# Windowed attention with a gated output layer on one core: global rows stored in one transfer per piece of columns, the last accumulator filled, copied and stored in two halves

## The chip, the cores and the metric

The kernel runs on one core of a Trainium2 chip. The metric is the device time of one execution in microseconds; of several runs the median counts.

## What is computed

For 8 batches and 8 heads of 64 channels there are 512 local tokens and 32 global ones. Local queries see local keys at a distance of at most 32 and all global keys; global queries see everything. The 8 heads' outputs stand side by side as x, with 512 columns and 32 + 512 rows per batch, and pass a gated layer:

```python
k_all = np.concatenate([k_g, k_l], axis=2)
out_g = np.matmul(sm(scale * np.matmul(q_g, k_all.transpose(0, 1, 3, 2))), v_all)
mask = np.abs(pos[:, None] - pos[None, :]) <= 32
...
x = concatenate([out_g, out_l], axis=2)   # then (batch, row, 512)
gate = sigmoid(sum_k conv_w[k] * x shifted down by 4 - k rows)
out = (gate * (x @ w_val)) @ w_out
```

The output has 8 batches of 544 rows of 512 f32. In each batch the first 32 rows belong to the global tokens.

## The kernel before

The work is cut into 32 units, one per batch and pair of heads. For each unit the tensor engine (PE) makes the scores, VectorE (DVE) their minima with the mask, ScalarE (ACT) the exponentials, PE transposes and multiplies by v; DVE and ACT then norm the result and build the gate from it. After four units a batch has all of x, and the function `moe` runs its layer: the tasks g1 (x times w_val, accumulators `pv`), gv (times the gate), gh and gl (the product split into a high and a low part), g2 (times w_out, accumulators `po`), ob (copy of a finished accumulator from PSUM to SBUF) and st (store to DRAM). Each matmul step is three matmuls, high by high, high by low and low by high, in a format that keeps enough bits of f32 together.

The rows of the global tokens of all 8 batches, 256 in number, are gathered in one tile and pass the layer in a last call of `moe` with the key "g". Its names in the profile end in g: `pvg`, `ghg`, `glg`, `pog`, `obg`. It has 48 matmuls of 256 columns in g1, and in g2 two accumulators of 128 rows by 512 columns, r = 0 and 1, with 12 matmuls of 512 columns each (line 643). Rows 0 to 31 of such an accumulator belong to one batch, 32 to 63 to the next, and so on, so four batches share one. A PSUM accumulator of 512 f32 columns comes from the pool's tag "mm", which has two buffers.

The first accumulator is copied by ScalarE alone (line 649). The last one is copied by ScalarE, left 256 columns, and by VectorE, right 256 columns (line 651). `store_g` (lines 834 to 836) then writes four pieces of 32 rows, one per batch, 64 KB each: two issued by SyncE (SP) and two by ScalarE, each queue one after the other. A transfer started on ScalarE's queue takes ScalarE's own time while it is issued.

What sets the order: the string ORDER lists the names of all tasks, and the program is emitted in just this order; each engine works off its instructions in the order in which they were emitted. The costs given to `plan.add` don't change the order. Semaphore waits are placed by the layer that records the program, from the tiles that an instruction reads and writes. The tail of ORDER is the last line of the string: `gl.g.2 gl.g.3 g2.g.0.1 ... g2.g.1.3 ob.g.1 st.g.1`.

Of the kernel before, what the change touches and what calls it, by code (L numbers as in the profile page):

```python
# [8 lines left out]
F32 = mybir.dt.float32  # L9
# [8 lines left out]
B, H, SL, SG, D = 8, 8, 512, 32, 64  # L18
DM = H * D
KW = 5  # L20
P = 128
NDT = DM // P
# [110 lines left out]
g2.7.2.2 st.7.1 gconv2 g2.7.2.3 gconv3 g2.7.3.0 ob.7.2 g2.7.3.1 g2.7.3.2 gconv1 g2.7.3.3 g1.g.0.0 gxl3 gconv0 ob.7.3  # L133
g1.g.0.1 g1.g.0.2 g1.g.0.3 g1.g.1.0 sigg g1.g.1.1 g1.g.1.2 gv.g.0 g1.g.1.3 gh.g.0 g1.g.2.0 gv.g.1 g1.g.2.1 g1.g.2.2
st.7.2 g1.g.2.3 gl.g.0 gv.g.2 gh.g.1 st.7.3 g1.g.3.0 gh.g.2 gl.g.1 g1.g.3.1 g1.g.3.2 g1.g.3.3 gv.g.3 gh.g.3 g2.g.0.0
gl.g.2 gl.g.3 g2.g.0.1 g2.g.0.2 g2.g.0.3 g2.g.1.0 ob.g.0 g2.g.1.1 st.g.0 g2.g.1.2 g2.g.1.3 ob.g.1 st.g.1
"""
E1 = D + 1
PW = "x"
# [6 lines left out]
WO = 2  # L146
NPC = 3
KEEP = 900
LAG = {"PE": 250, "ACT": 160, "DVE": 110, "POOL": 150, "SP": 100, "DMA": 2000, "FREE": 0}
OWN = {"ACT": 100, "DVE": 120}  # L150
PAIR = {("mx", "exp"): -490, ("exp", "t"): 150, ("tc", "av"): -350, ("mx", "mx"): 0, ("gmax", "gmax"): 0, ("halo", "conv"): 40, ("ob", "st"): 30}
# [7 lines left out]
def kind(name):  # L159
    return name.rstrip("0123456789.")  # L160
# [11 lines left out]
class Plan:  # L172
# [17 lines left out]
    def lag(self, d, t):  # L190
# [3 lines left out]
        eng = self.tasks[d].eng  # L194
        return PAIR.get((kind(d), kind(t.name)), OWN.get(eng, 0) if eng == t.eng else LAG[eng])

    def order(self):
# [7 lines left out]
        def put(t):  # L205
# [11 lines left out]
            if kind(t.name) in ("iq", "iv", "wi"):  # L217
                at = max(at, free["PE"] + LAG["PE"])
            if t.eng == "PE":
# [9 lines left out]
            for name, key in t.give:  # L229
                self.rings[name][2][key] = t.end + LAG[t.eng]  # L230
            line.append(t)
# [13 lines left out]
def attention_moe(ctx, tc, qk, vw, maskd, w_val, convT, w_out, out):  # L245
    nc = tc.nc
    V, A, G, T = nc.vector, nc.scalar, nc.gpsimd, nc.tensor

    cp = ctx.enter_context(tc.tile_pool(name="cp", bufs=1))
    sb = ctx.enter_context(tc.tile_pool(name="sb", bufs=2))  # L250
    ps = ctx.enter_context(tc.tile_pool(name="ps", bufs=1, space=PSUM))

    plan = Plan()
# [17 lines left out]
    wvh, wvl, woh, wol = (cp.tile([P, NDT, DM], F32R, name=n) for n in ("wvh", "wvl", "woh", "wol"))  # L271
# [36 lines left out]
    def on_pe(ins):  # L308
        last_pe[:] = [ins.ins]
# [156 lines left out]
    st = {}  # L466
# [137 lines left out]
    def sigmoid(g):  # L604
        A.activation(out=g, in_=g, func=AF.Sigmoid)
# [5 lines left out]
    def moe(key, n, x0, deps_x, deps_gate, before, store):  # L611

        box = {}
        last = before

        def g1(e, t):
            xh, xl = xs_h[x0 + t], xs_l[x0 + t]
            if t == 0:
                box["pv", e] = ps.tile([P, n], F32, tag="mm", name=f"pv{key}_{e}", bufs=2)
            for q, (w, x) in enumerate(((wvh, xh), (wvh, xl), (wvl, xh))):  # L620
                on_pe(T.matmul(box["pv", e], w[:, e, t * P:t * P + P], x, start=(t == 0 and q == 0),  # L621
                         stop=(t == NDT - 1 and q == 2)))

        def gv(e):
            if e == 0:
                box["gh"] = sb.tile([P, NDT, n], F32R, tag="gh", name=f"gh{key}", bufs=1)
                box["gl"] = sb.tile([P, NDT, n], F32R, tag="gl", name=f"gl{key}", bufs=1)
            box["gv", e] = sb.tile([P, n], F32, tag="gv", name=f"gv{key}_{e}")
            V.tensor_tensor(out=box["gv", e], in0=box["pv", e], in1=gates[x0 + e], op=ALU.mult)  # L629

        def gh(e):
            A.copy(box["gh"][:, e, :], box["gv", e])  # L632

        def gl(e):
            V.tensor_tensor(out=box["gl"][:, e, :], in0=box["gv", e], in1=box["gh"][:, e, :].bitcast(F32),
                            op=ALU.subtract)

        def g2(r, e):
            if e == 0:
                box["po", r] = ps.tile([P, DM], F32, tag="mm", name=f"po{key}_{r}", bufs=2)  # L640
            rs = slice(r * P, r * P + P)
            for q, (g, w) in enumerate(((box["gh"], woh), (box["gh"], wol), (box["gl"], woh))):
                on_pe(T.matmul(box["po", r], g[:, e, rs], w[:, e, :], start=(e == 0 and q == 0),  # L643
                         stop=(e == NDT - 1 and q == 2)))

        def ob(r):
            box["ob", r] = sb.tile([P, DM], F32, tag="ob", name=f"ob{key}_{r}")
            at = DM // 2 if (key, r) == ("g", n // P - 1) else DM
            A.copy(box["ob", r][:, :at], box["po", r][:, :at])  # L649
            if at < DM:  # L650
                V.tensor_copy(box["ob", r][:, at:], box["po", r][:, at:])

        part = 700 * n // 512 + (20 if n < 512 else 0)
        early = [f"pc{u}.{KW - 1}" for u in range(NPC)] if key == 0 else []
        for e in range(NDT):
            for t in range(NDT):
                name = f"g1.{key}.{e}.{t}"
                plan.add(name, "PE", part, lambda e=e, t=t: g1(e, t), [last, f"w{e}"] + deps_x(t) + early,
                         take=[("mm", name[:-2])] if t == 0 else [],
                         give=[("xh", x0 + t), ("xl", x0 + t)] if e == NDT - 1 else [])  # L660
                last = name
            plan.add(f"gv.{key}.{e}", "DVE", 620 * n // 512, lambda e=e: gv(e), [last] + deps_gate(e),
                     take=[("gv", f"{key}.{e}")] + ([("g", key)] if e == 0 else []),
                     give=[("mm", f"g1.{key}.{e}"), ("gate", x0 + e)])
            plan.add(f"gh.{key}.{e}", "ACT", 515 * n // 512, lambda e=e: gh(e), [f"gv.{key}.{e}"])
            plan.add(f"gl.{key}.{e}", "DVE", 610 * n // 512, lambda e=e: gl(e), [f"gh.{key}.{e}"], 
                     give=[("gv", f"{key}.{e}")], lock=True)
        for r in range(n // P):
            for e in range(NDT):
                name = f"g2.{key}.{r}.{e}"  # L670
                plan.add(name, "PE", 700, lambda r=r, e=e: g2(r, e),
                         [last, f"gl.{key}.{e}", f"w{NDT + e}"], take=[("mm", name[:-2])] if e == 0 else [],
                         give=[("g", key)] if (r, e) == (n // P - 1, NDT - 1) else [])
                last = name
            plan.add(f"ob.{key}.{r}", "ACT", 350 if (key, r) == ("g", n // P - 1) else 490, lambda r=r: ob(r), [last], take=[("ob", name[3:-2])],
                     give=[("mm", name[:-2])])
            plan.add(f"st.{key}.{r}", "ACT", 800 if key == "g" else 400, lambda r=r: store(r, box["ob", r]), [f"ob.{key}.{r}"])
            plan.add(f"sd.{key}.{r}", "DMA", 620, lambda: None, [f"st.{key}.{r}"], give=[("ob", f"{key}.{r}")])
        return last

# [32 lines left out]
    for kind_, n in first:  # L713
# [4 lines left out]
        if kind_ == "mask":  # L718
            arrival += 250
    plan.add("first", "DMA", arrival - LAG["DMA"], lambda: None)  # L720
    for k in range(2 * NDT):
# [8 lines left out]
    for u in range(NU):  # L730
        if ("qk", u) not in first:
            plan.add(f"iq{u}", "SP", 450, lambda u=u: load_qk(u), [f"iq{u - 1}"] if ("qk", u - 1) not in first else [],
                     take=[("qk", u)])
            plan.add(f"lq{u}", "DMA", 1600, lambda: None, [f"iq{u}"])
        if ("v", u) not in first:
            plan.add(f"iv{u}", "SP", 450, lambda u=u: load_v(u), [f"iq{u}"] if ("qk", u) not in first else [],
                     take=[("v", u)])
            plan.add(f"lv{u}", "DMA", 2350, lambda: None, [f"iv{u}"])

    for b in range(B):  # L740
        at = 0.04 * b
        units = range(NDT * b, NDT * b + NDT)
        plan.add(f"gs{b}", "PE", 1050, lambda b=b: g_s(b), [f"lq{u}" for u in units] + ([f"gs{b - 1}"] if b else []),
                 take=[("s", f"g{b}"), ("pt", f"ga{b}"), ("pt", f"gb{b}"), ("xg", b)])
        for h in range(2):
            n = f"{b}.{h}"
# [4 lines left out]
                     take=[("pt", f"gc{n}"), ("pt", f"gd{n}")], give=[("pg", n)])  # L751
# [3 lines left out]
                     take=[("pt", f"gv{n}")], give=[("pgt", n)])  # L755
# [6 lines left out]
    for u in range(NU):  # L762
        b, dt = divmod(u, NDT)
        at = 0.01 * u
        plan.add(f"s{u}", "PE", (1400, 1500)[u] if u < 2 else 1000, lambda u=u: l_s(u), [f"lq{u}"] + ([f"s{u - 1}"] if u else []),
                 take=[("s", u), ("pm", u), ("pts", u), ("mx", u)])
# [18 lines left out]
        if u < NPC:  # L785
            plan.add(f"dg{u}", "ACT", 1460, lambda u=u: diagonal(u), ["cw"] + ([f"dg{u - 1}"] if u else []),
                     take=diagonals(u)[0])
            for k in range(KW):
                plan.add(f"pc{u}.{k}", "PE", 880, lambda u=u, k=k: p_conv(u, k),
                         ([f"pc{u}.{k - 1}"] if k else [f"halo{u}", f"dg{u}"] + ([f"pc{u - 1}.{KW - 1}"] if u else [])),  # L790
                         take=[] if k else [("mm", f"pc{u}")], give=diagonals(u)[1] if k == KW - 1 else [])
            plan.add(f"conv{u}.{KW - 2}", "ACT", 480, lambda u=u: p_conv_out(u), [f"pc{u}.{KW - 1}", f"xl{u}"],
                     take=[("gate", u)], give=[("mm", f"pc{u}"), ("xc", u)])
        else:
            plan.add(f"tap{u}", *(("ACT", 520) if u < NTA else ("DVE", 400)), lambda u=u: l_tap(u), [f"xc{u}", "cw"],
                     take=[("gate", u)], lock=u >= NTA)
# [10 lines left out]
    last = "start"  # L807
    for b in range(B):
        units = range(4 * b, 4 * b + 4)
        for u in units:  # L810
            plan.add(f"sig{u}", "ACT", 530, lambda u=u: sigmoid(gates[u]),
                     [f"fix{v}" if v < NHF else f"conv{v}.{KW - 2}" for v in units] + ([f"sig{u - 1}"] if u % 4 else []))
        last = moe(b, SL, 4 * b, lambda t, b=b: [f"xl{4 * b + t}"], lambda e, b=b: [f"sig{4 * b + e}"], last,
                   lambda r, o, b=b: A.dma_start(out[b, SG + r * P:SG + r * P + P, :], o))

    def open_g():
        n = B * SG
# [13 lines left out]
    plan.add("sigg", "ACT", 1250, lambda: [sigmoid(gates[NU + dt]) for dt in range(NDT)],  # L831
             [f"gconv{dt}" for dt in range(NDT)])

    def store_g(r, o):
        for s in range(P // SG):
            (A if s % 2 else nc.sync).dma_start(out[r * (P // SG) + s, 0:SG, :], o[s * SG:s * SG + SG, :])

    moe("g", B * SG, NU, lambda t: [f"gxl{t}"], lambda e: ["sigg"], last, store_g)

    with tc.manual_schedule():  # L840
# [19 lines left out]
        for t in line:  # L860
            if t.eng == "PE":
                gap = t.start - clock["PE"]
                opened = opened or bool(t.take and t.take[0][0] == "mm")
                if not opened and gap > KEEP:
                    keep_clock(int((gap - 400) * 0.55 / 235))
# [65 lines left out]
```

## Time and profile before

| | |
|---|---|
| median of 3 runs | 372.37 us (372.1 to 372.75) |
| the profiled execution's own time | 372.69 us |
| its span, first to last instruction | 370.9 us |
| PE busy | 358.4 us, 97% of the span |
| DVE busy | 312.0 us, 84% |
| ACT busy | 257.2 us, 69% |
| granted TensorE clock, mean | 0.999 |
| stores of global rows | 8 transfers of 64 KB, 4 on SP and 4 on ACT |

Times inside the execution are in us from the start of the span. A row of a group or of the timeline names line, engine, operation, the tile written and the tiles read, and the shape; what stands in brackets after it is the time for which the engine had been idle and what ended that. Rows on SPq and ACTq are the issuing of transfers by SP and by ACT. PEld is the loading of weights, which can run beside a matmul. Ends of matmuls are modelled.

### The profile page before, as it was taken

What the parts mean: (1) busy time and instruction counts of PE and PEld (TensorE: products, weight loads), DVE (VectorE), ACT (ScalarE), POOL (GpSimd) and SP (SyncE); (2) the same over time, 40 slices, a digit from 0 to 9 for tenths busy, and PEclk for the clock granted to TensorE, in tenths of its full rate; (3) what the DMA queues carried; (4) which work ended last, traced back from release to release, by engine and by line L of the source; (5) the groups of instructions that cost most, each with busy time, mean ns of one, the idle gap of its engine ahead of it and who ended that gap; (6) DMA issues with size and microseconds to landing.
All of it is one profiled execution on the core that took longest, in us unless ns stands there. A gap on an engine that the chain in (4) does not pass through costs nothing.

```text
span 370.9 us, 14811 instructions
## 1 busy us (share of the span) xinstructions
PE 358.4 (97%) x6347; PEld 280.5 (76%) x6347; DVE 312.0 (84%) x1094; ACT 257.2 (69%) x620; POOL 0.9 (0%) x7
## 2 busy tenths in 40 slices
PE   7899899999999999999999999999999999999995
PEld 3556557877878787787877887788788888888894
DVE  4899999999998897998689968999768877684861
ACT  3898867976798676976886668977876568434231
POOL 0000000000000000000000000000000000000000
PEclk9999999999999999999999999999999999999999
DMA  8995686495667174881339361975853010011112
GB/s 288 398 340 199 212 302 229 158 357 177 198 218 269 49 267 111 304 310 78 129 120 358 128 195 74 323 220 188 268 214 110 4 58 30 30 57 59 55 61 57
DMA packets 17250, 66.74 MB, mean 180 GB/s; under 512 B 1952, under 2 KB 4000, under 8 KB 17184
## 3 DMA queue, kind: packets, MB, share of 16 engines
q1 hardware_dynamic: 12240, 57.12, 44.4%
q10 hardware_dynamic: 4944, 8.67, 6.4%
q8 instruction: 50, 0.82, 0.9%
q14 instruction: 16, 0.13, 0.1%
HBM read 56.87 MB, written 8.91 MB: 177 GB/s over the span
## 4 chain that ended last, share of the span: by engine, by line
PE 81%; DVE 9%; DMA 7%; issue 1%; ACT 1%; ACTq 0%
PE po L643 23%; PE pv L621 23%; PE ax L514 8%; PE pt L503 6%; PE sx L478 5%; PE ax L533 3%; DMA wraw<-in_w_val_dram 3%; DMA v<-in_vw_dram 2%; PE sy L478 2%; PE ag L446 2%; DVE pm L490 2%; PE pvg L621 2%; PE pog L643 1%; PE gs_sx L403 1%; PE gpt L426 1%; PE pc L597 1%
## 5 line engine op out<-in xcount | busy, mean ns | idle before, releaser
L497 ACT ACTIVATE pm<-pm,mx 128x128 f32<-128x128 f32 x256 | 80.8, 394 | 13.9 <-DVE mx L490 13.4
L572 DVE SCALAR_TENSOR_TENSOR gate<-xc,cw,gate 128x512 f32<-128x512 f32 x116 | 86.1, 748 | 1.4
L643 PE MATMUL po<-woh,gh 128*128 128x512 f32 x128 | 54.2, 424 | 0.5 <-issue 0.5
L621 PE MATMUL pv<-xh,wvh 128*128 128x512 f32 x128 | 54.5, 426 | 0.0
L621 PE MATMUL pv<-xl,wvh 128*128 128x512 f32 x128 | 50.4, 394 | 0.0
L643 PE MATMUL po<-woh,gl 128*128 128x512 f32 x128 | 50.3, 393 | 0.0
L621 PE MATMUL pv<-xh,wvl 128*128 128x512 f32 x128 | 50.2, 392 | 0.0
L643 PE MATMUL po<-wol,gh 128*128 128x512 f32 x128 | 50.1, 391 | 0.0
L506 ACT COPY pts<-pt 128x512 f32<-128x512 f32 x64 | 36.6, 587 | 15.8 <-PE pt L503 15.3
L514 PEld LDWEIGHTS ax<-v,pts 128*32 128x32 f32 x2048 | 30.6, 109 | 11.2 <-issue 3.7
L503 PE MATMUL pt<-ident,pm 128*128 128x128 f32 x256 | 37.3, 274 | 1.3 <-DVE mx L521 0.6
L478 PE MATMUL sx<-qk 64*32 64x128 f32 x1024 | 38.0, 274 | 0.3 <-DVE mx L490 0.3
L503 PEld LDWEIGHTS pt<-ident,pm 128*128 128x128 f32 x256 | 30.5, 140 | 10.2 <-ACT pm L497 1.9
L478 PE MATMUL sy<-qk 64*32 64x128 f32 x1024 | 36.8, 274 | 0.5 <-DVE mx L490 0.4
L514 PE MATMUL ax<-v,pts 128*32 128x65 f32 x2048 | 35.7, 221 | 1.5 <-ACT pts L506 1.4
L478 PEld LDWEIGHTS sx<-qk 64*32 64x32 f32 x1024 | 28.7, 105 | 8.4 <-issue 3.6
L490 DVE CUSTOM_DVE_ANT_0 pm<-sx,mask 128x128 f32<-128x128 f32 x128 | 29.4, 286 | 4.1 <-PE sx L478 4.1
L632 ACT CAST gh<-gv 128x512 fp32r<-128x512 f32 x32 | 19.6, 622 | 18.2 <-DVE gv L629 15.9
L649 ACT COPY ob<-po 128x512 f32<-128x512 f32 x32 | 18.7, 584 | 18.5 <-PE po L643 18.4
L629 DVE TENSOR_TENSOR gv<-pv,gate 128x512 f32<-128x512 f32 x32 | 22.0, 687 | 10.8 <-PE pv L621 10.7
L537 ACT COPY xc<-ax 128x512 f32<-128x512 f32 x32 | 18.9, 589 | 15.4 <-DVE gate L572 12.9
L490 DVE CUSTOM_DVE_ANT_0 pm<-sy,mask 128x128 f32<-128x128 f32 x128 | 29.4, 286 | 0.0
(114 smaller groups left out, 653.4 us busy)
## 6 DMA issues: line engine op xcount, KB each, us to landing
v<-in_vw_dram SPq DMA_DIRECT2D x32, 975.0 KB, 6.7
qk<-in_qk_dram SPq DMA_DIRECT2D x32, 624.0 KB, 4.3
out_dram<-ob ACTq DMA_DIRECT2D x32, 256.0 KB, 2.4
wraw<-in_w_val_dram SPq DMA_DIRECT2D x4, 512.0 KB, 12.3
wraw<-in_w_out_dram SPq DMA_DIRECT2D x4, 512.0 KB, 4.6
mask<-in_mask_dram SPq DMA_DIRECT2D x1, 256.0 KB, 4.4
out_dram<-obg SPq DMA_DIRECT2D x4, 64.0 KB, 1.7
out_dram<-obg ACTq DMA_DIRECT2D x4, 64.0 KB, 2.0
```

The costliest lines, as they stand in the source:

```text
L478: on_pe(T.matmul((sx, sy)[h][32 * j:32 * j + 32, i, :], qkt[rows, 32 * m:32 * m + 32], qkt[rows, k0:k0 + P], start=True, stop=True))
L490: V.tensor_tensor_reduce(out=pm[:, h, i, :], in0=s[:, i, :], in1=mask[:, i, :], op0=ALU.add, op1=ALU.min, scale=-SCALE, scalar=3.0e38, acc ...
L497: A.activation(out=pm[:, h, i, :], in_=pm[:, h, i, :], func=AF.Exp, bias=mx[:, c:c + 1], scale=-1.0)
L503: on_pe(T.transpose(pt[:, i, :], pm[:, h, i, :], ident))
L506: A.copy(st[u]["pts"][:, h], st[u]["pt", h])
L514: on_pe(T.matmul(ax[32 * j:32 * j + 32, h, E1 * i:E1 * i + E1], pts[:, h, i, 32 * j:32 * j + 32], vt[:, block_win(4 * i + j), h, :], start ...
L537: A.copy(xc[:, KW - 1:], flat(u)[:, SL:])
L572: V.scalar_tensor_tensor(out=acc, in0=xc[:, k:k + SL], scalar=cw[:, u % NDT, k:k + 1], in1=acc, op0=ALU.mult, op1=ALU.add)
L621: on_pe(T.matmul(box["pv", e], w[:, e, t * P:t * P + P], x, start=(t == 0 and q == 0), stop=(t == NDT - 1 and q == 2)))
L629: V.tensor_tensor(out=box["gv", e], in0=box["pv", e], in1=gates[x0 + e], op=ALU.mult)
L632: A.copy(box["gh"][:, e, :], box["gv", e])
L643: on_pe(T.matmul(box["po", r], g[:, e, rs], w[:, e, :], start=(e == 0 and q == 0), stop=(e == NDT - 1 and q == 2)))
```

## The change

Three things are changed, all in the call of `moe` for the global rows.

1. `store_g` takes a list of pieces, each a queue and a range of columns, and issues one transfer for each: 4 batches by 32 rows by the columns. The first accumulator's 256 KB are one transfer on ScalarE's queue.
2. The 12 matmuls of the last accumulator (the key END) become 24 of 256 columns: first all 12 for the left half, then all 12 for the right half. A new task `half` stands in ORDER between them: ScalarE copies the left half and stores it (128 KB).
3. When the right half is done, ScalarE copies and stores columns 256 to 383, VectorE copies columns 384 to 511 and SP stores them, 64 KB each.

In ORDER st.g.0 moves ahead of g2.g.1.1, and `half` comes behind it.

```diff
-gl.g.2 gl.g.3 g2.g.0.1 g2.g.0.2 g2.g.0.3 g2.g.1.0 ob.g.0 g2.g.1.1 st.g.0 g2.g.1.2 g2.g.1.3 ob.g.1 st.g.1
+gl.g.2 gl.g.3 g2.g.0.1 g2.g.0.2 g2.g.0.3 g2.g.1.0 ob.g.0 st.g.0 g2.g.1.1 half g2.g.1.2 g2.g.1.3 ob.g.1 st.g.1
...
+HALF = DM // 2
+END = ("g", B * SG // P - 1)
...
             if e == 0:
                 box["po", r] = ps.tile([P, DM], F32, tag="mm", name=f"po{key}_{r}", bufs=2)
             rs = slice(r * P, r * P + P)
-            for q, (g, w) in enumerate(((box["gh"], woh), (box["gh"], wol), (box["gl"], woh))):
-                on_pe(T.matmul(box["po", r], g[:, e, rs], w[:, e, :], start=(e == 0 and q == 0),
-                         stop=(e == NDT - 1 and q == 2)))
+            cols, es = slice(0, DM), [e]
+            if (key, r) == END:
+                cols, es = slice(e // 2 * HALF, e // 2 * HALF + HALF), [e % 2 * 2, e % 2 * 2 + 1]
+            for e in es:
+                for q, (g, w) in enumerate(((box["gh"], woh), (box["gh"], wol), (box["gl"], woh))):
+                    on_pe(T.matmul(box["po", r][:, cols], g[:, e, rs], w[:, e, cols], start=(e == 0 and q == 0),
+                             stop=(e == NDT - 1 and q == 2)))
 
         def ob(r):
+            if (key, r) != END:
+                box["ob", r] = sb.tile([P, DM], F32, tag="ob", name=f"ob{key}_{r}")
+                A.copy(box["ob", r], box["po", r])
+                return
+            at = HALF + HALF // 2
+            A.copy(box["ob", r][:, HALF:at], box["po", r][:, HALF:at])
+            V.tensor_copy(box["ob", r][:, at:], box["po", r][:, at:])
+
+        def first_half(r):
+
             box["ob", r] = sb.tile([P, DM], F32, tag="ob", name=f"ob{key}_{r}")
-            at = DM // 2 if (key, r) == ("g", n // P - 1) else DM
-            A.copy(box["ob", r][:, :at], box["po", r][:, :at])
-            if at < DM:
-                V.tensor_copy(box["ob", r][:, at:], box["po", r][:, at:])
+            A.copy(box["ob", r][:, :HALF], box["po", r][:, :HALF])
+            store(r, box["ob", r], ((A, 0, HALF),))
...
-            plan.add(f"ob.{key}.{r}", "ACT", 350 if (key, r) == ("g", n // P - 1) else 490, lambda r=r: ob(r), [last], take=[("ob", name[3:-2])],
+            if (key, r) == END:
+                plan.add("half", "ACT", 720, lambda r=r: first_half(r), [name[:-1] + "1"], take=[("ob", name[3:-2])])
+            plan.add(f"ob.{key}.{r}", "ACT", 240 if (key, r) == END else 490, lambda r=r: ob(r),
+                     [last] + (["half"] if (key, r) == END else []), take=[] if (key, r) == END else [("ob", name[3:-2])],
                      give=[("mm", name[:-2])])
-            plan.add(f"st.{key}.{r}", "ACT", 800 if key == "g" else 400, lambda r=r: store(r, box["ob", r]), [f"ob.{key}.{r}"])
+            parts = ((A, HALF, HALF + HALF // 2), (nc.sync, HALF + HALF // 2, DM)) if (key, r) == END else ((A, 0, DM),)
+            plan.add(f"st.{key}.{r}", "ACT", 400, lambda r=r, parts=parts: store(r, box["ob", r], parts), [f"ob.{key}.{r}"])
             plan.add(f"sd.{key}.{r}", "DMA", 620, lambda: None, [f"st.{key}.{r}"], give=[("ob", f"{key}.{r}")])
...
-                   lambda r, o, b=b: A.dma_start(out[b, SG + r * P:SG + r * P + P, :], o))
+                   lambda r, o, parts, b=b: A.dma_start(out[b, SG + r * P:SG + r * P + P, :], o))
...
-    def store_g(r, o):
-        for s in range(P // SG):
-            (A if s % 2 else nc.sync).dma_start(out[r * (P // SG) + s, 0:SG, :], o[s * SG:s * SG + SG, :])
+    def store_g(r, o, parts):
+        n = P // SG
+        for queue, a, z in parts:
+            queue.dma_start(out[r * n:r * n + n, 0:SG, a:z], o[:, a:z])
```

What it does to the order on PE, at the last accumulator (`pog_6292`; `ghg` and `glg` are the two parts of the gated product, `woh` and `wol` those of w_out). Before, the last six of its twelve matmuls; what stands in brackets are the waits:

```order
L643 MATMUL pog_6292<-woh,ghg 128x512
L643 MATMUL pog_6292<-wol,ghg 128x512
L643 MATMUL pog_6292<-woh,glg 128x512
L643 MATMUL pog_6292<-woh,ghg 128x512
L643 MATMUL pog_6292<-wol,ghg 128x512
L643 MATMUL pog_6292<-woh,glg 128x512
```

Now, the last three of the left half and the first three of the right half:

```order
L649 MATMUL pog_6292<-woh,ghg 128x256
L649 MATMUL pog_6292<-wol,ghg 128x256
L649 MATMUL pog_6292<-woh,glg 128x256
L649 MATMUL pog_6292<-woh,ghg 128x256 [waits Activation_49]
L649 MATMUL pog_6292<-wol,ghg 128x256
L649 MATMUL pog_6292<-woh,glg 128x256
```

The 13th matmul, the first of the right half, now has a wait for ScalarE's semaphore; before, none of the twelve had one.

On ACT, at the end of the program, before (`obg_6296` is the copy of the first accumulator, `obg_6311` that of the last):

```order
L649 COPY obg_6296<-pog_6277 128x512 [waits DMAHW0_49,PE_49]
L836 DMA out_dram<-obg_6296 32x512 [waits Activation_49]
L836 DMA out_dram<-obg_6296 32x512
L649 COPY obg_6311<-pog_6292 128x256 [waits DMAHW1_49,PE_49]
L836 DMA out_dram<-obg_6311 32x512 [waits DVE_49]
L836 DMA out_dram<-obg_6311 32x512
```

And now (`obg_6299` and `obg_6308`):

```order
L655 COPY obg_6299<-pog_6277 128x512 [waits DMAHW0_49,PE_49]
L855 DMA out_dram<-obg_6299 4x32x512 [waits Activation_49]
L664 COPY obg_6308<-pog_6292 128x256 [waits DMAHW1_49,PE_49]
L855 DMA out_dram<-obg_6308 4x32x256 [waits Activation_49]
L658 COPY obg_6308<-pog_6292 128x128 [waits PE_49]
L855 DMA out_dram<-obg_6308 4x32x128 [waits Activation_49]
```

ScalarE has two copies of the last accumulator in place of one, and one store behind each copy in place of two. VectorE's copy of the last accumulator, now 128 columns, still waits for ScalarE's semaphore, as before. On SP the four stores become one, of 128 columns, at the very end. Nothing ahead of st.g.0 moves on any engine.

## The prediction

> **What bounds the kernel now.** I read the page first, for who is busy and for the chain of waits over the whole span.
>
> ```profile
> PE 358.4 (97%) x6347; PEld 280.5 (76%) x6347; DVE 312.0 (84%) x1094; ACT 257.2 (69%) x620; POOL 0.9 (0%) x7
> ...
> PE 81%; DVE 9%; DMA 7%; issue 1%; ACT 1%; ACTq 0%
> ```
>
> The tensor engine (PE) is busy 97% of the span and is 81% of the chain, so the kernel as a whole is bound by matmuls. The change touches none of that until the last two accumulators. What counts is therefore the end, and I asked for the chain of waits in the last 16 us. Its columns are start, length and what.
>
> ```profile
> 355.65 5.65 PE pvg L621 x48
> 361.30 5.46 PE pog L643 x24
> 366.77 0.02 issue
> 366.79 0.38 ACT obg L649
> 367.17 0.03 issue
> 367.20 0.42 DVE obg L651
> ```
>
> The matmuls run without a gap up to 366.77. After that nothing overlaps any more: ScalarE's copy of the left half, then VectorE's copy of the right half, one after the other. The timeline of the end shows who starts what (start, length, engine, line):
>
> ```profile
> 366.37 0.39 PE L643 MATMUL pog<-woh,glg 128*128 128x512 f32 x1
> 366.79 0.37 ACT L649 COPY obg<-pog 128x256 f32<-128x256 f32 x1 [2.13 <-PE pog L643]
> 367.20 0.42 DVE L651 COPY obg<-pog 128x256 f32<-128x256 f32 x1 [4.53 <-ACT obg L649]
> 367.65 0.78 SPq L836 DMA_DIRECT2D out_dram<-obg  x2
> 367.65 0.85 ACTq L836 DMA_DIRECT2D out_dram<-obg  x2
> ```
>
> VectorE's copy reads other columns than ScalarE's and still waited for it: its idle time ended with `ACT obg`. Then each queue issues two transfers of 64 KB. The answer on line 836 gives the length of an issue (min/median/max ns) and the time from issue to landing:
>
> ```profile
> L836 SPq DMA_DIRECT2D out_dram<-obg x4: 315/385/414, 364.7 to 368.0; - x4
> L836 ACTq DMA_DIRECT2D out_dram<-obg x4: 375/410/441, 364.7 to 368.1; - x4
> DMA to landing us min/median/max: 1.6/1.9/2.0
> ```
>
> Last, the stages of the end; the last two columns are the busy share of the DMA engines and GB/s:
>
> ```profile
> 366.60:368.40 1.80, 0.15 (x1) 0.00 (x0) 0.42 (x1) 0.37 (x1) 0.00 (x0) 1.00 0.01 3
> 368.40:369.60 1.20, 0.00 (x0) 0.00 (x0) 0.00 (x0) 0.00 (x0) 0.00 (x0) 1.00 0.86 219
> 369.60:370.90 1.30, 0.00 (x0) 0.00 (x0) 0.00 (x0) 0.00 (x0) 0.00 (x0) 0.82 0.00 0
> ```
>
> For 1.8 us the DMA engines are idle, then the 256 KB go out, then nothing moves for 1.3 us: receipt of the last transfer and the closing barriers. So the end is a chain: last matmul over at 366.76; two copies; two issues in a row, the second starting at 367.65 + 0.41 = 368.06; landing at most 2.0 later, at about 370.0; and 0.9 us of closing work that the change doesn't touch.
>
> **The change, term by term.** (a) Narrower matmuls. Twelve matmuls of 512 columns become 24 of 256. Both widths stand in the chain above: 5.65 / 48 = 0.118 us each for 256 columns with new weights every time, 5.46 / 24 = 0.228 for 512. The whole costs 24 x 0.118 - 12 x 0.228 = +0.10 us. This is on the path.
>
> (b) The wait in the middle. The program order shown with the change has a wait for ScalarE on the 13th narrow matmul. What it waits for is the copy of the left half, since no other ScalarE work stands between. PE has nothing else left, so this wait is exposed. Where its times start:
>
> ```profile
> 361.02 0.28 PE L621 MATMUL pvg<-xgh,wvl 128*128 128x256 f32 x1
> ...
> 363.87 0.39 PE L643 MATMUL pog<-woh,ghg 128*128 128x512 f32 x1
> ```
>
> The last accumulator starts at 363.87 in both kernels. Its 12th narrow matmul starts 11 x 0.118 = 1.30 later and takes 0.28, so it ends at 365.45. ScalarE starts 0.03 later (366.76 to 366.79 above), copies 256 columns in 0.37 and is done at 365.85. How soon PE then goes on, an earlier place shows where it sat waiting for ScalarE:
>
> ```profile
> 12.02 1.06 ACT L506 COPY pts<-pt 128x512 f32<-128x512 f32 x2
> ...
> 13.14 0.16 PEld L514 LDWEIGHTS ax<-v,pts 128*32 128x32 f32 x8 [1.27 <-ACT pts L506]
> 13.14 0.26 PE L514 MATMUL ax<-v,pts 128*32 128x65 f32 x4 [0.95 <-ACT pts L506]
> ```
>
> From 13.08 to 13.14 is 0.06, which gives 365.91. Without a wait the 13th would have started at 363.87 + 12 x 0.118 = 365.29, so the wait costs 0.62 us. A load of weights that can no longer hide behind a matmul can come on top:
>
> ```profile
> 360.91 0.19 PEld L621 LDWEIGHTS pvg<-xgh,wvl 128*128 128x128 f32 x1
> ```
>
> That is between 0 and 0.19; I take 0.05, near the lower end, because in the row at 13.14 matmul and load start together. The term is 0.67 us, between 0.62 and 0.81. Cover there is none, as PE's earlier work is all done.
>
> Against this change speaks a rule of the Trainium skill, page "PSUM — Partial Sum Buffer", section "PSUM bank collisions raise a hardware error": no two engines may touch one PSUM bank in the same partitions at once, even at different columns, so guards go by bank and not by address. An accumulator of 512 f32 columns is one bank by that page. The trace agrees as far as it goes: the VectorE copy of other columns ended a wait of 4.53 us on ScalarE. By the rule the wait of (b) is needed and costs the 0.67; if columns could be told apart it would be 0, and the sum below would end at -0.70 instead of -0.03.
>
> (c) Copies and issues at the end. ScalarE and VectorE now copy 128 columns each, still one after the other, since both read the accumulator the wait above was about. Rows of that size from PSUM:
>
> ```profile
> L437 ACT COPY pgt<-gpt 128x128 f32<-128x128 f32 x16 | 4.4, 273 | 0.0
> L490 DVE CUSTOM_DVE_ANT_0 pm<-sx,mask 128x128 f32<-128x128 f32 x128 | 29.4, 286 | 4.1 <-PE sx L478 4.1
> ```
>
> So 0.27 and 0.29 in place of 0.37 and 0.42; the VectorE row is another operation on the same shape, and the 0.42 of the wider copy is its upper end. From the last matmul to the last issue: 0.03 + 0.27 + 0.03 + 0.29 + 0.03 = 0.65. Before it was 368.06 - 366.76 = 1.30, because each queue had a second issue to make. Saved: 0.65 us, at least 0.52.
>
> (d) Landing. The last transfer before was the second of its queue, with three others under way, and I read the 2.0 for it. The last one after is alone on SP, with ScalarE's quarter issued about 0.32 earlier on the same DMA engines. The left half, issued near 365.9, is out long before. The rows give 1.6 to 2.0; I take 1.85, since it has one neighbour and not three. Saved 0.15. But its pieces are now 128 of 512 B, not 32 of 2 KB. What the trace has for 128 pieces, and for short ones:
>
> ```profile
> q1 hardware_dynamic: 12240, 57.12, 44.4%
> q10 hardware_dynamic: 4944, 8.67, 6.4%
> ...
> out_dram<-ob ACTq DMA_DIRECT2D x32, 256.0 KB, 2.4
> wraw<-in_w_val_dram SPq DMA_DIRECT2D x4, 512.0 KB, 12.3
> wraw<-in_w_out_dram SPq DMA_DIRECT2D x4, 512.0 KB, 4.6
> ```
>
> A packet of q1 has 4.67 KB on average and takes 0.444 x 16 x 370.9 / 12240 = 0.215 us; one of q10 has 1.75 KB and takes 0.077. Time goes with bytes, with no visible share per packet, so 512 B pieces should be no worse. The upper end is a store of 128 pieces of 2 KB, 2.4 us, which would turn the saving into a loss of 0.4.
>
> The Trainium skill, page "DMA: Bandwidth & Descriptors", section "Anatomy of one DMA — SWDGE (gpsimd) path", puts one transfer at a constant of about 2.0 us plus its bytes at 436 GB/s, for transfers issued by another engine. By that an estimate for 64 KB is 2.15 and the sum would be +0.27. The row's 1.6 to 2.0 for the same size is below it and decides here.
>
> (e) The first accumulator's store becomes one transfer on ScalarE's queue, and SP's two issues there go. ScalarE is idle 2.13 us ahead of its last copy in the row above, of which the issues took 0.85, and the SP queue has nothing else to do. The copy of the left half comes at 365.48, after the single issue has ended near 365.1. Cost nothing; if that issue took over 0.8 us instead of some 0.4, the rest would add to (b).
>
> The sum: +0.10 + 0.67 - 0.65 - 0.15 = -0.03 us. The gain at the end is about what the wait takes. The profiled execution took 372.69 us, 0.32 above the median of the three runs shown, 372.37; from the median the change gives 372.34, written 372.3. The low end of the terms is -0.03 - 0.05 - 0.25 (landing 1.6) = -0.33. The high end is -0.03 + 0.14 (weights) + 0.13 (copy) + 0.55 (landing 2.4) = +0.79.
>
> **Rivals.** First, slower: the short pieces bring the last transfer's landing far down the list. The loads from w_val come in pieces of 1 KB out of long rows, those from w_out in whole rows of the same total, and they landed in 12.3 against 4.6 us. At that ratio, 2.7, the 1.85 becomes 4.9, +3.1 us, or 375.4. It decides from a landing of about 2.6 us on, +0.78. Against it: the first w_val loads share the start of the kernel with the other first loads, and time by packet goes with bytes in both queues. 0.1.
>
> Second, faster: the wait in the middle is not paid, because the 13th matmul's wait is met by earlier ScalarE work or the copy can run under the matmuls. Then the sum lacks 0.67 and ends at 371.7, right at the edge of what can be told. With a landing of 1.6 it is 371.4. For it speaks only that a row of the order doesn't carry the awaited count; against it, that VectorE's copy of other columns was held in the same way. 0.08.
>
> **How the numbers follow.** The forecast, both sides cancel, has 0.82; 0.2%, about 0.75 us, is the least that a measurement of this kernel can tell from no change, and both ends of the likely terms lie inside or at it. The upper tail, weights and landing both at their high ends, is part of the slower chance: 0.1 for the first rival and 0.01 for that tail. Of the second rival's 0.08 nearly all is faster; 0.01 comes from measuring. So faster 0.09, same 0.8, slower 0.11. For the range I add the spread of the runs, 0.3 either way, to the low end, which gives 371.8; at the high end I stop at 373.0, short of all bounds coming together.
>
> **What would show it.** In the profile after: 24 narrow matmuls 0.118 apart, in two runs of 12; between them a gap of 0.6 to 0.8 us from start to start, ended by ScalarE's copy; last matmul over near 367.5; VectorE's last copy again right behind ScalarE's, some 0.29 long; SP's single issue near 368.2; span end near 370.9. Wrong I would be if PE shows no gap, if the two last copies overlap, or if SP's transfer lands later than 2.4 us or sooner than 1.6 us after its issue.

## The result

The changed kernel takes 376.53 us (median of 4 runs, 376.33 to 376.79), beside 372.38 us for the kernel before on the same chip. The ratio is 1.0109, with an interval from 1.0096 to 1.0121: slower by 4.06 us by the ratio, where no change was forecast. The profiled execution took 376.79 us, with a span of 375.0 us; before it was 372.69 and 370.9. So the trace holds the loss: 4.1 us of span.

The matmuls are as busy as ever, 358.7 us against 358.4. The loss lies at the end. This is the timeline of the changed kernel's ScalarE from the first global accumulator's copy on (start, length, engine, line, what; in brackets the idle time before and what ended it):

```profile
364.21 0.59 ACT L655 COPY obg<-pog 128x512 f32<-128x512 f32 x1 [1.87 <-PE pog L649]
364.83 1.14 ACTq L855 DMA_DIRECT2D out_dram<-obg  x1
366.06 0.37 ACT L664 COPY obg<-pog 128x256 f32<-128x256 f32 x1 [1.27 <-PE pog L649]
366.47 0.55 ACTq L855 DMA_DIRECT2D out_dram<-obg  x1
368.22 0.27 ACT L658 COPY obg<-pog 128x128 f32<-128x128 f32 x1 [1.78 <-PE pog L649]
368.52 0.55 ACTq L855 DMA_DIRECT2D out_dram<-obg  x1
```

And this is the same stretch on the tensor engine (the first matmul of the last accumulator, the 12th, the 13th and the 24th), with VectorE's copy and SP's issue behind it:

```profile
364.01 0.28 PE L649 MATMUL pog<-woh,ghg 128*128 128x256 f32 x1
...
365.32 0.28 PE L649 MATMUL pog<-woh,glg 128*128 128x256 f32 x1
366.49 0.38 PE L649 MATMUL pog<-woh,ghg 128*128 128x256 f32 x1 [0.89 <-ACT obg L664]
...
367.90 0.28 PE L649 MATMUL pog<-woh,glg 128*128 128x256 f32 x1
...
368.52 0.29 DVE L659 COPY obg<-pog 128x128 f32<-128x128 f32 x1 [5.71 <-ACT obg L658]
368.84 0.70 SPq L855 DMA_DIRECT2D out_dram<-obg  x1
```

The gap between the two halves is there, ended by ScalarE's copy as forecast, but it is 1.17 us from start to start. The copy that ends it began at 366.06, although the 12th matmul was over at 365.60: ScalarE's queue was still issuing the first accumulator's store, 1.14 us long, until 365.97.

SP's issue begins at 368.84, only 0.78 us later than the last issue before (368.06). But from there to the end of the span it is 6.16 us, and was 2.84. The stages of the end show why (the last two columns are the busy share of the DMA engines and GB/s):

```profile
365.40:366.40 1.00, 0.20 (x2) 0.00 (x0) 0.00 (x0) 0.34 (x1) 0.00 (x0) 1.00 0.07 16
366.40:369.00 2.60, 1.69 (x12) 1.49 (x12) 0.29 (x1) 0.30 (x2) 0.00 (x0) 1.00 0.24 43
369.00:373.00 4.00, 0.00 (x0) 0.00 (x0) 0.00 (x0) 0.00 (x0) 0.00 (x0) 1.00 0.27 91
373.00:374.00 1.00, 0.00 (x0) 0.00 (x0) 0.00 (x0) 0.00 (x0) 0.00 (x0) 0.54 0.11 32
374.00:375.00 1.00, 0.00 (x0) 0.00 (x0) 0.00 (x0) 0.00 (x0) 0.00 (x0) 0.50 0.00 0
```

From 366.4 to 373 the DMA share stays near a quarter, 0.24 to 0.27 of 16 engines, or four engines. Before, the last 256 KB went out at a share of 0.86. From 369 on the engines that work aren't slower: 91 / (0.27 x 16) = 21 GB/s each, against 219 / (0.86 x 16) = 16 before. There are too few of them, and the share stays at a quarter while packets of both queues are under way, so the trace speaks for the same four for all. All 512 KB of global rows (16 + 112 + 364 + 32 = 524 thousand bytes by the rows) pass through them, until about 373.7.

The first stretch has a second trouble. This is one microsecond of it:

```profile
367.00:368.00 1.00, 1.00 (x10) 0.98 (x9) 0.00 (x0) 0.00 (x0) 0.00 (x0) 1.00 0.18 27
```

Here a working engine moves only 27 / (0.18 x 16) = 9 GB/s. The trace has packets of 2 KB that took up to 0.97 us near 367, and 0.084 us later. At 21 GB/s each, four engines would carry the 524 thousand bytes in 6.2 us; by the packets they took 7.6, from 366.1 to 373.7. Why the first packets are slow stays open.

The loss in parts: the last accumulator starts 0.14 later (364.01 for 363.87); from there to the last matmul's end it is 4.17 us where it was 2.89, so 1.28 more (1.14 for the wait, since from the 12th start to the last it is 2.58 us and 12 x 0.12 = 1.44 would do, and 0.14 for the narrow form); from the last matmul's end to the last issue it is 0.66 where it was 1.30, a saving of 0.64; from the last issue to the end it is 3.32 more. The sum is 0.14 + 1.28 - 0.64 + 3.32 = +4.10, as by the spans. The 0.14 lies ahead of the place where the change begins; this start differs as much among the other runs.

### The profile page after: what moved, and what is told of

Same layout as the page of the kernel before. It is cut to its first block, busy times and chain, and to the rows that moved or that the text cites. A ratio compares the mean times of both kernels' runs of the same rounds, so it can differ in the third digit from the quotient of the medians.

```text
span 375.0 us, 14831 instructions
## 1 busy us (share of the span) xinstructions
PE 358.7 (96%) x6359; PEld 281.2 (75%) x6359; DVE 311.7 (83%) x1094; ACT 257.6 (69%) x621; POOL 0.8 (0%) x7
## 4 chain that ended last, share of the span: by engine, by line
PE 77%; DVE 15%; DMA 4%; issue 1%; ACT 1%; ACTq 0%
PE po L649 23%; PE pv L623 23%; PE ax L516 7%; PE pt L505 6%; PE sx L480 4%; DMA wraw<-in_w_val_dram 3%; PE ax L535 3%; DVE pm L492 2%; PE sy L480 2%; PE ag L448 2%; PE pvg L623 2%; DVE gate L574 1%; PE gs_sx L405 1%; PE gpt L428 1%; PE pog L649 1%
```

## The experiments

Theory A: the outermost dimension of a store sets how many DMA engines share it. A store of 4 batches by 32 rows gets four engines, and all merged stores get the same four. Rivals: B, the shape of the transfers itself (pieces of 512 B, a dimension more) makes them slow; C, the halves and their wait are what costs; D, the longer issue on ScalarE's queue is. The first four kernels ran on one chip in 3 rounds, the kernel before at 372.43 us; the other four in 5 rounds, at 372.69 us. Ratios are to the kernel before on the same chip.

**outer16: 16 outermost instead of 4.** The rows of an accumulator are put in another order, token by token with the 8 batches inside, so that one store covers 16 tokens of 8 batches. The merging, the halves and the 512 B pieces stay.

```diff
-        hv, lv, acc = (h[NU + dt].rearrange("p (b q) -> p b q", b=B) for h in (xs_h, xs_l, gates))
+        hv, lv, acc = (h[NU + dt].rearrange("p (q b) -> p b q", b=B) for h in (xs_h, xs_l, gates))
...
-        n = P // SG
+        n = P // B
...
-            queue.dma_start(out[r * n:r * n + n, 0:SG, a:z], o[:, a:z])
+            queue.dma_start(out[:, r * n:r * n + n, a:z].rearrange("b q c -> q b c"), o[:, a:z])
```

> The changed kernel with one thing altered: the global rows are ordered row by row and then batch by batch (in the three tiles that the global gather fills), so that each of the four stores has 16 rows by 8 batches by columns in place of 4 batches by 32 rows. Number of stores, bytes, piece lengths (2 KB, 1 KB, 512 B), halves and waits stay. Theory A (the count of the outermost dimension, 4, is the count of DMA engines that move a store): share of the DMA engines near 0.9 while data moves, the first store's issue back from 1.14 to about 0.4 us, time 372.2 to 372.8 us. Theory B (short pieces, or a pattern of three dimensions, are slow whatever the outer count): 376.0 to 376.6 us. Theory C (the halves and their wait cost the time): 376.0 to 376.6 us.

It took 378.75 us, ratio 1.0165 (1.0149 to 1.018): slower than the changed kernel, and as a test of the time a miss for A. The trace says where the time went. The first row is the group of VectorE's gate convolutions in this kernel, the second the same group in the kernel before (min/median/max ns), the third ScalarE's waiting in this kernel:

```profile
L714 DVE SCALAR_TENSOR_TENSOR gateg<-xgT,cw,gateg x16: 677/724/770, 348.0 to 361.0; 128x256 f32<-128x256 f32 x16
```

```profile
L696 DVE SCALAR_TENSOR_TENSOR gateg<-xgT,cw,gateg x16: 483/485/488, 347.4 to 356.4; 128x256 f32<-128x256 f32 x16
```

```profile
ACT gateg L607 <- DVE gateg L714: 5.3, 1, 5.3
```

The edit made VectorE read and write the gate with a stride, and each of its convolutions took 724 ns in place of 485. ScalarE waited 5.3 us for the gates, and the last matmul ended at 372.1 instead of 368.2. So the edit broke something ahead of the place it was to test. What it says about the stores themselves can still be read. They have a time from issue to landing again, and the DMA engines are no longer at a quarter (the last window of the transfers of this kernel):

```profile
out_dram<-obg ACTq DMA_DIRECT2D x1, 256.0 KB, 3.0
out_dram<-obg ACTq DMA_DIRECT2D x1, 128.0 KB, 2.4
out_dram<-obg ACTq DMA_DIRECT2D x1, 64.0 KB, 2.0
out_dram<-obg SPq DMA_DIRECT2D x1, 64.0 KB, 2.1
```

```profile
373.40:374.60 1.20, 0.00 (x0) 0.00 (x0) 0.00 (x0) 0.00 (x0) 0.00 (x0) 1.00 0.44 109
```

SP's issue began at 372.75 and the span ended at 375.8: 3.05 us, where the changed kernel takes 6.16. Two of A's other signs were off: the first issue took 0.66 us and not about 0.4, and the share was 0.62 from 370 to 371.9 us and not near 0.9. The time had to be tested again without the strided writes (outer16_rows, below).

**halves_per_batch: the halves without the merging.** Each piece is stored by one transfer per batch, on SP and ScalarE in turn as before, and the right half as one piece of 256 columns.

```diff
-            parts = ((A, HALF, HALF + HALF // 2), (nc.sync, HALF + HALF // 2, DM)) if (key, r) == END else ((A, 0, DM),)
+            parts = ((A, HALF, DM),) if (key, r) == END else ((A, 0, DM),)
...
-            queue.dma_start(out[r * n:r * n + n, 0:SG, a:z], o[:, a:z])
+            for s in range(n):
+                (A if s % 2 else nc.sync).dma_start(out[r * n + s, 0:SG, a:z], o[s * SG:s * SG + SG, a:z])
```

> The changed kernel with halves, but every store cut into one transfer for each batch again, two on SP and two on ACT; the right half is stored in pieces of 256 columns once both copies are done. Theory A: each transfer has an outer count of 32, all engines work; the last matmul ends 0.8 us later than in the kernel before, copies and second issue take 1.05, landing 2.0: 372.6 to 373.2 us. Theory B: pieces of 1 KB remain short, so 373.5 to 376 us. Theory C: 376.0 to 376.6 us.

It took 373.18 us, ratio 1.0017 (1.0008 to 1.0027). So the halves, without merging, cost about 0.6 us. That refutes C as the main cause and lies in A's range. The answer on the store's line has six issues on each queue, of the length that they had before, and landings as before:

```profile
L856 SPq DMA_DIRECT2D out_dram<-obg x6: 315/384/472, 364.7 to 368.8; - x6
L856 ACTq DMA_DIRECT2D out_dram<-obg x6: 374/408/444, 364.7 to 368.8; - x6
DMA to landing us min/median/max: 1.5/1.7/2.0
```

**merged_only: the merging without the halves.** The kernel before, with the four stores of an accumulator made one of 4 by 32 by 512 on ScalarE's queue. Its pieces are 2 KB, as before.

```diff
-        for s in range(P // SG):
-            (A if s % 2 else nc.sync).dma_start(out[r * (P // SG) + s, 0:SG, :], o[s * SG:s * SG + SG, :])
+        n = P // SG
+        A.dma_start(out[r * n:r * n + n, 0:SG, :], o)
```

> The kernel before with its accumulators and copies, but each accumulator's 256 KB stored in one transfer on ACT, 4 batches by 32 rows by 512 columns. Theory A: two transfers of 32 pieces of 0.134 us on each of 4 engines, 4.3 us each, one behind the other from 365.9 on, so the data ends near 374.5 and the time is 377.0 to 377.8 us. Theory B by short pieces: whole rows are not short, one issue is saved, 371.8 to 372.4 us. Theory C: no halves, 371.8 to 372.4 us.

It took 376.56 us, ratio 1.0122 (1.0093 to 1.0151). With neither halves nor short pieces it is as slow as the changed kernel, though below A's 377.0 to 377.8 us. These are its stages behind the first store's issue, then the issues of its two stores:

```profile
365.60:369.00 3.40, 0.85 (x4) 0.38 (x2) 0.42 (x1) 0.37 (x1) 0.00 (x0) 1.00 0.24 54
369.00:372.60 3.60, 0.00 (x0) 0.00 (x0) 0.00 (x0) 0.00 (x0) 0.00 (x0) 0.71 0.25 86
372.60:374.70 2.10, 0.00 (x0) 0.00 (x0) 0.00 (x0) 0.00 (x0) 0.00 (x0) 0.50 0.04 14
```

```profile
364.38 1.15 ACTq L836 DMA_DIRECT2D out_dram<-obg  x1
...
367.35 0.55 ACTq L836 DMA_DIRECT2D out_dram<-obg  x1
```

The share is a quarter again, 0.24 and 0.25. The long issue is here too, 1.15 us, but nobody waits for it: it ended at 365.53, and the next copy came well behind that, at 366.49. So D does not make this kernel slow.

**first_per_batch: only the first accumulator unmerged.** The changed kernel, with the first accumulator's store cut into four again.

```diff
-            queue.dma_start(out[r * n:r * n + n, 0:SG, a:z], o[:, a:z])
+            if r == 0:
+                for s in range(n):
+                    (A if s % 2 else nc.sync).dma_start(out[r * n + s, 0:SG, a:z], o[s * SG:s * SG + SG, a:z])
+            else:
+                queue.dma_start(out[r * n:r * n + n, 0:SG, a:z], o[:, a:z])
```

> The changed kernel, but the first accumulator stored as before in four transfers, two on SP and two on ACT; the last accumulator as changed. Theory A: the copy of the left half starts near 365.5 again and the four engines are free of the first 256 KB, so only 1.5 us of left half and 1.7 us of quarters remain for them: 373.3 to 374.0 us. Theory B: the last two transfers are slow by themselves and stay so: 375.0 to 376.2 us. Theory C: 375.5 to 376.6 us.

It took 373.98 us, ratio 1.0042 (1.0027 to 1.0057). Its stages show both kinds of store, one behind the other:

```profile
365.40:366.60 1.20, 0.64 (x5) 0.64 (x6) 0.00 (x0) 0.37 (x1) 0.00 (x0) 1.00 0.89 219
366.60:368.20 1.60, 1.06 (x9) 0.85 (x8) 0.21 (x1) 0.27 (x1) 0.00 (x0) 1.00 0.15 38
368.20:371.00 2.80, 0.00 (x0) 0.00 (x0) 0.08 (x1) 0.00 (x0) 0.00 (x0) 1.00 0.24 72
```

The first accumulator's four stores go out at a share of 0.89, the merged ones of the last at 0.24. The ratios put the loss in parts: 4.06 for the whole change; 1.56 with the first accumulator unmerged; 0.63 with both. So the merging of the first accumulator costs about 2.5 us, that of the last 0.9, the halves 0.6; by the intervals the first two are uncertain by some 0.7 us each, the third by 0.4. The first store, which the prediction had at no cost, is the largest part: its 256 KB stand on the four engines ahead of the last accumulator's.

**outer16_rows: 16 outermost, with nothing slowed ahead.** As outer16, but the convolution's input is kept in the same order of rows, so that VectorE reads and writes without a stride.

```diff
-    xgT = cp.tile([P, NDT, B, KW - 1 + SG], F32, name="xgT")
+    xgT = cp.tile([P, NDT, KW - 1 + SG, B], F32, name="xgT")
...
-        A.copy(xgT[:, :, b, KW - 1:], xt.rearrange("p (c q) -> p c q", c=NDT))
+        A.copy(xgT[:, :, KW - 1:, b], xt.rearrange("p (c q) -> p c q", c=NDT))
...
-        hv, lv, acc = (h[NU + dt].rearrange("p (b q) -> p b q", b=B) for h in (xs_h, xs_l, gates))
+        hv, lv, acc = (h[NU + dt].rearrange("p (q b) -> p q b", b=B) for h in (xs_h, xs_l, gates))
...
-            queue.dma_start(out[r * n:r * n + n, 0:SG, a:z], o[:, a:z])
+            queue.dma_start(out[:, r * n:r * n + n, a:z].rearrange("b q c -> q b c"), o[:, a:z])
```

> The changed kernel with stores of 16 rows by 8 batches by columns, as in the run with the reordered rows, but now the gathered tile of global tokens itself is kept row by row, so that VectorE reads and writes without gaps and nothing ahead of the last accumulators gets slower. Halves, waits, number of stores and piece lengths as changed. Theory A (outer count = number of DMA engines): all 16 engines work, the last store lands 2.1 us after its issue near 368.2, 372.4 to 372.9 us. Theory B (the pattern of three dimensions or the pieces of 512 B cost the time): 375.5 to 376.6 us. Theory D (the merged stores cost by their longer issue alone, 0.55 to 1.15 us each): 373.5 to 374.5 us.

It took 373.22 us, ratio 1.0013 (1.0001 to 1.0024): 0.5 us over the kernel before, and 3.6 under the changed one by the ratios. One store per piece, halves, 512 B pieces and a third dimension are all still there; the outermost dimension went from 4 to 16, and the one inside it from 32 to 8. B is refuted. The time is 0.3 us above A's range and 0.3 below D's, so by itself it doesn't decide between these two. The end of its timeline, two of its stages and the last store's landing:

```profile
365.04 0.66 ACTq L855 DMA_DIRECT2D out_dram<-obg  x1
365.54 0.28 PE L649 MATMUL pog<-woh,glg 128*128 128x256 f32 x1
...
365.86 0.37 ACT L664 COPY obg<-pog 128x256 f32<-128x256 f32 x1 [0.84 <-PE pog L649]
366.28 0.39 PE L649 MATMUL pog<-woh,ghg 128*128 128x256 f32 x1 [0.46 <-ACT obg L664]
366.50 0.28 PE L649 MATMUL pog<-wol,ghg 128*128 128x256 f32 x1
...
367.70 0.28 PE L649 MATMUL pog<-woh,glg 128*128 128x256 f32 x1
...
368.63 0.67 SPq L855 DMA_DIRECT2D out_dram<-obg  x1
```

```profile
365.70:368.00 2.30, 1.82 (x14) 1.50 (x12) 0.00 (x0) 0.37 (x1) 0.00 (x0) 1.00 0.60 156
...
369.30:370.50 1.20, 0.00 (x0) 0.00 (x0) 0.00 (x0) 0.00 (x0) 0.00 (x0) 1.00 0.44 109
...
out_dram<-obg SPq DMA_DIRECT2D x1, 64.0 KB, 2.1
```

Here the terms of the prediction can be read one by one. The issue of the first store is over at 365.70, before the left half is (365.82), and the copy follows at once. From the 12th start to the last it is 2.16 us, 0.72 over the 1.44 without a wait. From the last matmul's end (367.98) to SP's issue it is 0.65. From there to the end of the span (371.7) it is 3.07, with a landing of 2.1.

**even_odd: 8 outermost.** The changed kernel, with every second row of the global tokens in an accumulator, so that a store has 8 batches of 16 rows.

```diff
-            rs = slice(r * P, r * P + P)
+            rs = slice(r, 2 * P, 2) if key == "g" else slice(r * P, r * P + P)
...
-            queue.dma_start(out[r * n:r * n + n, 0:SG, a:z], o[:, a:z])
+            queue.dma_start(out[:, r:SG:2, a:z], o[:, a:z])
```

> The changed kernel, but accumulator r holds the global rows 2p + r (the weights of its matmuls are every second column), so each store is 8 batches by 16 rows by columns. Number of stores, bytes, piece lengths, halves and waits as changed. Theory A: 8 engines work, share 0.5 while data moves, half of the time on the engines as with 4: 372.9 to 373.8 us. Theory B (dimensions or pieces, whatever the outer count): 375.5 to 376.6 us, share 0.25. Theory D: 373.5 to 374.5 us with a share near 0.9.

It took 373.53 us, ratio 1.0035 (1.0019 to 1.005). That lies in A's range, but also in D's, and its interval overlaps that of outer16_rows; what tells the theories apart is the share, 0.5 by A and near 0.9 by D. Its stages:

```profile
365.60:368.00 2.40, 1.71 (x12) 1.51 (x12) 0.28 (x1) 0.29 (x2) 0.00 (x0) 1.00 0.45 118
368.00:369.00 1.00, 0.00 (x0) 0.00 (x0) 0.01 (x1) 0.00 (x0) 0.00 (x0) 1.00 0.24 79
369.00:370.20 1.20, 0.00 (x0) 0.00 (x0) 0.00 (x0) 0.00 (x0) 0.00 (x0) 1.00 0.41 106
```

The DMA share is up to 0.45 here, close to the half that 8 of 16 engines can reach. The first issue takes 1.21 us in this kernel, as long as with 4 outermost, and the time is still some 2.8 us below the changed kernel's: D is not the main cause.

A share of a quarter could also be sixteen engines that are each busy a quarter of the time. The packets of the traces speak against that. Besides the rows, every store has packets of 4 bytes near its end: 16 for each store of 32 rows in the kernel before, 4 for each merged store in the changed kernel and in merged_only, 8 for each one here, 16 in outer16_rows. These are just the numbers of engines that A gives.

**outer16_whole: merging alone, with 16 outermost.** The kernel before with the order of rows of outer16_rows and no halves: each accumulator has two stores of 16 by 8 by 256, the left on ScalarE, the right on SP.

```diff
-        for s in range(P // SG):
-            (A if s % 2 else nc.sync).dma_start(out[r * (P // SG) + s, 0:SG, :], o[s * SG:s * SG + SG, :])
+        n = P // B
+        for queue, a in ((A, 0), (nc.sync, DM // 2)):
+            z = a + DM // 2
+            queue.dma_start(out[:, r * n:r * n + n, a:z].rearrange("b q c -> q b c"), o[:, a:z])
```

> No halves in the matmuls: the kernel before, rows kept row by row, each accumulator stored in two transfers of 16 rows by 8 batches by 256 columns, the left one on ACT right behind ScalarE's copy, the right one on SP behind VectorE's. Theory A: no wait of 0.67 on PE, one issue for each queue, last issue at 367.7, landing 2.1 to 2.4: 372.0 to 372.6 us. Theory B: 375 us or more. Theory C (the halves are what costs): 372.0 to 372.4 us.

It took 372.7 us, ratio 1.0004 (0.9993 to 1.0015): no difference from before, and 0.1 us above A's range. This is the end of its timeline:

```profile
366.22 0.37 ACT L649 COPY obg<-pog 128x256 f32<-128x256 f32 x1 [2.13 <-PE pog L643]
366.62 0.56 ACTq L838 DMA_DIRECT2D out_dram<-obg  x1
366.63 0.42 DVE L651 COPY obg<-pog 128x256 f32<-128x256 f32 x1 [4.53 <-ACT obg L649]
367.08 0.55 SPq L838 DMA_DIRECT2D out_dram<-obg  x1
```

ScalarE's store now goes out while VectorE still copies, and each queue has one issue. Merging as such costs nothing here once all engines share the store, and it gains nothing that could be measured.

**outer16_banks: the right half in its own PSUM tile.** As outer16_rows, so that the 13th matmul has no copy to wait for.

```diff
+                if (key, r) == END:
+                    box["right"] = ps.tile([P, DM], F32, tag="sx", name="right")
...
-                    on_pe(T.matmul(box["po", r][:, cols], g[:, e, rs], w[:, e, cols], start=(e == 0 and q == 0),
+                    on_pe(T.matmul((box["right"] if cols.start else box["po", r])[:, cols], g[:, e, rs], w[:, e, cols], start=(e == 0 and q == 0),
...
-            A.copy(box["ob", r][:, HALF:at], box["po", r][:, HALF:at])
-            V.tensor_copy(box["ob", r][:, at:], box["po", r][:, at:])
+            A.copy(box["ob", r][:, HALF:at], box["right"][:, HALF:at])
+            V.tensor_copy(box["ob", r][:, at:], box["right"][:, at:])
```

> The changed kernel with stores of 16 rows by 8 batches and with the right half of the last accumulator in a PSUM tile of its own, so that its matmuls have nothing of ScalarE's to wait for. If the wait on ScalarE is the term of 0.67 us that the prediction gave it, this kernel is 0.5 to 0.8 us faster than the one with the same stores and one tile: 371.7 to 372.2 us; if PE's gap has another cause, the two are within 0.2 us.

It took 372.27 us, ratio 0.9987 (0.9978 to 0.9996). This is its timeline around the two halves:

```profile
365.57 0.28 PE L651 MATMUL pog<-woh,glg 128*128 128x256 f32 x1
365.69 0.28 PE L651 MATMUL right<-woh,ghg 128*128 128x256 f32 x1
365.89 0.37 ACT L666 COPY obg<-pog 128x256 f32<-128x256 f32 x1 [0.85 <-PE pog L651]
...
367.01 0.28 PE L651 MATMUL right<-woh,glg 128*128 128x256 f32 x1
```

The 13th matmul starts 0.12 us behind the 12th, and from the 12th to the last it is 1.44 us instead of 2.16: the wait of 0.72 us is gone, and ScalarE's copy runs under the matmuls. The medians of the two kernels are 0.95 us apart, a little more than the 0.72 and than the 0.5 to 0.8 that was expected. This version beats both kernels, the one before by 0.13% (0.04 to 0.22).

## Why the prediction was wrong

(a) Narrower matmuls, +0.10: nearly right, 0.14 by the rows. 24 of them come 0.12 us apart in all kernels with halves.

(b) The wait in the middle, +0.67 (0.62 to 0.81): the mechanism was right and so was the size where nothing else disturbs it, 0.72 us in outer16_rows. The matmul behind the wait took 0.39 us and the next started 0.22 behind it, instead of 0.12, so 0.10 us more than the 0.62 came on top; that this is the weight load, of which 0.05 was forecast, is not shown. In the changed kernel the term is 1.14, for the reason in (e). The rule of the Trainium skill that was weighed there, on the page "PSUM — Partial Sum Buffer", agrees with outer16_banks, where with a tile of its own for the right half the same matmul has no wait. No run left the wait out with one tile for both halves, so that the chip needs it is not shown here.

(c) Copies and issues, -0.65: right. From the last matmul's end to the last issue it is 0.66 us in the changed kernel and 0.65 in outer16_rows, as worked out.

(d) Landing, -0.15: this is the step that failed, +3.32, together with the "Cost nothing" of (e), on which it rests. "The left half, issued near 365.9, is out long before" was wrong: from 366.4 to 373 all merged stores stood in line on four engines. By the packets of the trace the first accumulator's store was out at 370.84 and the left half at 372.20, and SP's last store, issued at 368.84, moved its first row at 372.07. Why this one, in a queue of its own, began no earlier is not shown. The bytes and their pieces were counted, not the engines that would carry them. The 2.4 us of another store of 128 pieces was taken as the upper end, but that store is written with 128 rows outermost and this one with 4 batches. Where a merged store has all 16 engines, as in outer16_rows, the landing is 2.1 us and the end comes 0.23 us later than before: even then not a saving.

A page of the Trainium skill that the prediction cited for another purpose has the rule that was missed: "DMA: Bandwidth & Descriptors", section "Why a DMA increments its semaphore by 16 and not by 1". It says that a transfer's engines are the largest number up to 16 that divides the slowest dimension, not of size 1, of both its patterns, and that from SP and ScalarE they are always the lowest-numbered ones. By it 4 batches by 32 rows get four engines, the same four on both queues. The traces agree: a share of 0.24 to 0.27 with 4 outermost, up to 0.45 with 8, 0.60 over a whole stage with 16. Which numbers the engines have, the rows do not show.

(e) The first accumulator's store: "Cost nothing; if that issue took over 0.8 us instead of some 0.4, the rest would add to (b)." The zero was wrong, and the condition behind it came true. The issue took 1.14 us and held ScalarE's copy back by 0.43 us (366.06 instead of 365.63), which is nearly all that (b) exceeded 0.72 by. And its bytes, on four engines, were what the last accumulator's stores stood behind: 2.5 us with the issue, by first_per_batch.

The first rival named a late last landing and a time of 375.4 us, near the measured one, but for a cause that the runs refute: merged_only has pieces of 2 KB and is slow, outer16_rows has pieces of 512 B and is not. The second rival, no wait in the middle, did not occur; outer16_banks made it happen, and by its trace it is worth 0.72 us, near the 0.67 that was said.

The sum without the failed step was near: with 16 outermost the measured terms are 0.14 + 0.72 - 0.65 + 0.23 = +0.44 us, and outer16_rows is 0.48 us over the kernel before by its ratio (0.04 to 0.89), where -0.03 was forecast.

## What to carry to other kernels

When several stores are merged into one, look at the outermost dimension of the merged pattern before counting bytes: here 4 outermost left 12 of 16 DMA engines idle and cost about 3.4 us, while the same bytes with 16 outermost cost nothing that could be measured. Read the DMA share of the stage, not only the bytes: a quarter that stays constant while both queues have work is a sign of it. And the copy of one half of an accumulator ran under the matmuls of the other only once each half had a PSUM tile of its own; with one tile for both, a wait of 0.72 us took back more than the earlier store gained.

## What was not expected

The issue of a merged store is longer than that of a plain one, 0.55 to 0.77 us against 0.32 to 0.47, and the first merged one with 4 or 8 outermost takes twice that, 1.14 to 1.21 us, though 0.66 with 16. Why the first differs stays open; no run was made for it. Where the last accumulator's stores alone are merged, it is the first of these that is long, so it is not the first accumulator as such:

```profile
365.94 1.15 ACTq L859 DMA_DIRECT2D out_dram<-obg  x1
...
368.31 0.69 SPq L859 DMA_DIRECT2D out_dram<-obg  x1
```

Reading and writing f32 with a stride of 8 elements made a VectorE operation on 128x256 half as long again, 724 ns instead of 485 (one that only writes so took 464 instead of 348), enough to put 3.9 us on the end of a kernel that had seemed bound by matmuls there.
